# Where the rows 129 to 256 of an expert are divided, and when the last expert's first rows are written, in a second mixture of experts

## The chip, the core and the metric

The kernel runs on one core of one Trainium2 chip. The metric is device time in microseconds (us), the median over runs. One more execution was recorded by the hardware profiler, and all rows below are of it.

## The reference

Attention with two masks (local and strided) gives 1152 rows of 512 numbers. Two mixtures of experts follow. The first sends each row to its two best experts of eight. The second, which the change touches, sends each row to one expert and drops what is over the capacity:

```
expert_idx = np.argmax(logits, axis=1)
...
h = np.maximum(np.einsum('ecd,edf->ecf', disp, w1), 0.0)     # disp: (8, 288, 512), w1: (8, 512, 1024)
y = np.einsum('ecf,efd->ecd', h, w2)                         # w2: (8, 1024, 512)
...
out[i] = gate_w[i] * y[expert_idx[i], pos[i]]
```

How many rows an expert gets is known only when the kernel runs.

## The kernel before

Five engines take part. TensorE (PE) multiplies, ScalarE (ACT) and VectorE (DVE) move and divide data, GpSimd (POOL) issues the gathers and scatters of rows, and SyncE (SP) issues the loads of weights. Each works through its own queue in program order; the order in the code is written out by hand.

**Divided numbers.** To come near fp32 with a faster matmul type, each operand is divided into a high part `hi` and a remainder `lo`, and each product is three matmuls: hi x hi, lo x hi, hi x lo (`mm3`, line 905). For the weights, ACT writes `hi` (line 77) and DVE writes `lo` (line 82), after which SP may load the chunk six places further on into the freed buffer (line 68). For the gathered rows, `x_turn` (line 411) transposes them on PE into a PSUM bank, and `x_split` (line 421) divides the bank: ACT writes `hi` (line 423), then DVE writes `lo` (line 424), both into the tile `xt`.

**Blocks.** An expert's rows come in blocks of 128, 128 and 32 (`nb2`). `block(e, b, ...)` (line 934) is one block's two layers, 24 matmuls of 512 columns for each (`up` and `down`), with a transposition of the hidden layer between them (`h_turn`, lines 918, 920, 921). Block 0 is always computed. Blocks 1 and 2 stand in an If at line 997 and one at line 1004, and are computed where the expert has more than 128 or 256 rows. Every engine passes these Ifs on its own. Where a block is skipped, each engine still steps the semaphores that the block would have stepped. In this run the experts 1, 2, 4 and 7 have a block 1, and expert 2 has a block 2; 0, 3, 5 and 6 have block 0 alone.

**Order in the common part.** `first_block(e)` (line 955) holds what is done for every expert. Between the two layers PE turns the rows of this expert's block 1 into bank 5 and those of the next expert's block 0 into bank 6. In the second layer, at step 2, ACT and DVE divide the next expert's block 0 (line 981). At the steps 3 to 6 they divide four chunks of the next expert's weights (line 983). This expert's block 1 is divided only inside the If (line 998), so that in the queues of ACT and DVE it stands behind those four chunks. For the last expert there are no four chunks.

**Writing.** `put_rows(e, b, ps)` (line 923) scales a block's rows on ACT (line 925), clears a spacer on POOL (line 926) and scatters the rows to the output with an indirect DMA (line 927). An expert's block 0 is put at the start of the next expert's common part. The last expert's block 0 is put at the very end (line 1017), behind its block 1.

**Expert 0.** Behind its common part DVE decodes the lists of rows (`L2.decode()`, lines 505 to 508), and POOL then gathers the rows of expert 2 (line 1015) into a tile that the trace names `hot`. PE turns these in the common part of expert 1.

Of the kernel before, what the change touches and what calls it, by code (L numbers as in the profile page):

```python
# [21 lines left out]
DM, FF, E = 512, 1024, 8  # L22
# [16 lines left out]
def blocks(n):  # L39
    return [(a, min(128, n - a)) for a in range(0, n, 128)]  # L40
# [3 lines left out]
def attention_moe_moe_kernel(ctx: ExitStack, tc: tile.TileContext, a, out, capacity):  # L44
# [35 lines left out]
    def split_lo(i, eng):  # L80
        if i < len(chunks):
            eng.tensor_tensor(lo[i % SPLIT], raw[i % RAW], hi[i % SPLIT].bitcast(F32), op=OP.subtract)  # L82
            load(i + RAW)

    def split(eng=None):
        split_lo(split_hi(), eng or dve)
# [261 lines left out]
    bank = [banks[:, i] for i in range(8)]  # L348
# [30 lines left out]
    def count_ranks(sb, first, last):  # L379

        ps = bank[7][:, :(NT + 1) * E].rearrange("p (c e) -> p c e", e=E)
        pe.matmul(ps[:, :NT, :], tri, sb, start=first, stop=False, skip_group_check=True)
        pe.matmul(ps[:, NT, :], ones, sb[:, NT - 1, :], start=False, stop=False,
                  skip_group_check=True)
        for c in range(NT - 1):
            n = NT - c
            pe.matmul(ps[:, c + 1:NT + 1, :], ones, sb[:, c, None, :].to_broadcast([128, n, E]),
                      start=False, stop=last and c == NT - 2, skip_group_check=True)
        return ps
# [14 lines left out]
    def gather(xg, src, ix, n, only=(0, 1, 2)):  # L404
        for b, (s0, m) in enumerate(blocks(n)):
            if b not in only:
                continue
            pool.indirect_dma_start(out=xg[:m, b, :src.shape[1]], out_offset=None, in_=src,  # L408
                                    in_offset=bass.IndirectOffsetOnAxis(ap=ix[:m, b:b + 1], axis=0))

    def x_turn(xg, b, m, ps=None):
        ps = (ps or next_bank("tr")).rearrange("p (d s) -> p d s", d=4)
        for d in range(4):
            pe.transpose(ps[:, d, :m], xg[:m, b, d * 128:(d + 1) * 128], ident[:m, :m])  # L414
        return ps

    def x_cols(xg, xs, b, m, s0=None, ps=None):

        x_split(x_turn(xg, b, m, ps), xs, b * 128 if s0 is None else s0, m)

    def x_split(ps, xs, s0, m):
        h, l = (x[:, :, s0:s0 + m] for x in xs)
        act.copy(h, ps[:, :, :m])  # L423
        dve.tensor_tensor(l, ps[:, :, :m], h.bitcast(F32), op=OP.subtract)
# [110 lines left out]
    ps = count_ranks(ohb[:, 1], False, True)  # L535
# [311 lines left out]
    nb2 = blocks(c2)  # L847
# [7 lines left out]
    xs2, hs2 = ([t[:, :, i * c2:(i + 1) * c2] for i in range(2)] for t in (xt, ht))  # L855
# [34 lines left out]
    def has(e, b):  # L890
        return (more_blocks >> (2 * e + b - 1)) & 1

    def tell(e, b):
        tc.mark_branch_hint_location(f"block{e}_{b}", hint=has(e, b), engines=engines)  # L894

    pending = [split_hi() for _ in range(4)]
    ps = []
# [25 lines left out]
    def put_rows(e, b, ps):  # L923
        m = nb2[b][1]
        act.activation(rows[e % 2][:m, b, :DM], ps[:m], AF.Copy, scale=L2.g(e, b, m))  # L925
        pool.memset(spacer, 0.0)  # L926
        i = pool.indirect_dma_start(  # L927
            out=out, out_offset=bass.IndirectOffsetOnAxis(ap=L2.ix[:m, e, b:b + 1], axis=0),
            in_=rows[e % 2][:m, b, :DM], in_offset=None, bounds_check=T - 1, oob_is_err=False)
        for k in put:  # L930
            tc.declare_no_dep(i.ins, k.ins, reason="rows of other tokens")
        put.append(i)

    def block(e, b, out_bank, also):

        ci = 64 + 8 * e
        s0, m = nb2[b]
        x, hc = ([t[:, :, s0:s0 + m] for t in u] for u in (xs2, hs2))
        also("start")
        for j in range(2):  # L940
            ps = bank[2 + j]
            for k in range(4):
                mm3(ps[:m], [t[:, k] for t in x], wide(ci + 2 * j, k), k == 0, k == 3)
                if j and k == 1:
                    also("up")
                    h_turn(b, 0)
            act.activation(h[:m, j * 512:j * 512 + 512], ps[:m], AF.Relu)
        also("between")
        for k in range(8):
            mm3(out_bank[:m], [t[:, k] for t in hc], wide(ci + 4, k), k == 0, k == 7)  # L950
            if k == 1:
                h_turn(b, 1)
            also(k)

    def first_block(e):
        def two(n=2):
            for _ in range(n):
                if e == 0 and pending:
                    split_lo(pending.pop(0), dve)
                else:  # L960
                    split()

        def also(at):
            if at == "start":
                if e:
                    two()
                    put_rows(e - 1, 0, bank[0] if e % 2 else bank[7])
                    if e + 2 < E:
                        gather(xg[(e + 2) % 3], acc, L2.ix[:, e + 2], c2)
            elif at == "up":  # L970
                if e:
                    two(1)
            elif at == "between":
                if e:
                    two(1)
                if len(nb2) > 1:
                    s.append(x_turn(xg[e % 3], 1, nb2[1][1], bank[5]))
                if e + 1 < E:
                    s.append(x_turn(xg[(e + 1) % 3], 0, nb2[0][1], bank[6]))
            elif at == 2 and e + 1 < E:  # L980
                x_split(s[-1], xs2, 0, nb2[0][1])
            elif at in (3, 4, 5, 6) and e + 1 < E:
                two(1)

        s = []
        block(e, 0, bank[7] if e % 2 else bank[0], also)
        return s[0] if len(nb2) > 1 else None

    def other_blocks(e, ps):

        def also(at):
            if at == "between" and len(nb2) > 2:
                x_cols(xg[e % 3], xs2, 2, nb2[2][1], ps=bank[6])

        if len(nb2) == 1:
            return
        with tc.If(has(e, 1) > 0, preferred_fallthrough_block=True, label=f"block{e}_1"):  # L997
            x_split(ps, xs2, 128, nb2[1][1])
            if len(nb2) > 2:
                tell(e, 2)  # L1000
            block(e, 1, bank[5], also)
            put_rows(e, 1, bank[5])
            if len(nb2) > 2:
                with tc.If(has(e, 2) > 0, preferred_fallthrough_block=True, label=f"block{e}_2"):  # L1004
                    block(e, 2, bank[6], lambda at: None)
                    put_rows(e, 2, bank[6])

    put = []
    for e in range(E):
        if len(nb2) > 1:  # L1010
            tell(e, 1)
        ps = first_block(e)
        if e == 0:
            L2.decode()
            gather(xg[2], acc, L2.ix[:, 2], c2)
        other_blocks(e, ps)
    put_rows(E - 1, 0, bank[7])


_NAMES = {"w1": "moe_w1", "w2": "moe_w2", "v1": "moe2_w1", "v2": "moe2_w2"}  # L1020
# [96 lines left out]
```

## Time and profile before

| | us |
|---|---|
| runs without the profiler, median of 3 | 554.35 (553.63 to 555.62) |
| the profiled execution's own time | 556.55 |
| its span, first to last instruction | 554.7 |
| PE busy in the span | 509.5 (92%) |
| second mixture, first matmul of block 0 of expert 0 to last of block 1 of expert 7 | 352.7 to 542.8 |

Times in rows are counted from the start of the span. A row of the timeline has its start, its duration (of several equal instructions together, with their count as x2), engine, line, operation and operands; in brackets stands how long the engine was idle before it, and what ended that. An engine's name with a q (ACTq, POOLq) is its sequencer. The ends of matmuls are modelled and overlap; from start to start of two matmuls is the better measure. PEclk is the granted clock of PE as a share of 2.4 GHz: 1.00, or 0.50, which is 1.2 GHz.

### The profile page before, as it was taken

Reading aid. Unit: us, or ns where it says so; the run is one execution under the profiler, and the core shown is the slowest. Engines: PE = TensorE matmul, PEld = TensorE weight load, DVE = VectorE, ACT = ScalarE, POOL = GpSimd, SP = SyncE. Lnnn points to the kernel's source line nnn. Section 1 sums busy time; section 2 is a strip of 40 time slices with the busy share of each in tenths; the row PEclk is TensorE's granted clock in tenths of the full one; section 3 lists DMA queues with packets and bytes.
Section 4 is the critical chain, followed back from the end, with each engine's and each line's share of the span. In section 5 each row is a group of like instructions: output and inputs, shape, how many; then the busy total and the mean of one; then the engine's idle time right before and its main releaser. Section 6 shows DMA issues by size and latency. Waiting matters only on the chain. (4 is left out here: it accounts for less than half of the span.)

```text
span 554.7 us, 9506 instructions
## 1 busy us (share of the span) xinstructions
PE 509.5 (92%) x3367; PEld 434.8 (78%) x3367; DVE 297.1 (54%) x662; ACT 269.5 (49%) x520; POOL 166.6 (30%) x216
## 2 busy tenths in 40 slices
PE   6899779999999999999999999897989999899991
PEld 3777569999999999999999995665767577677770
DVE  5498458755555555555554546175171068348820
ACT  4487345544544636454454623254371177257810
POOL 1244047826123050605030126753040043041001
PEclk9699858999999999999999996998997999899996
DMA  9988666847767576847666474359082069449400
GB/s 198 212 253 248 240 205 216 294 151 188 232 174 224 210 205 209 205 152 169 202 150 168 140 198 69 91 211 327 33 269 109 20 218 353 157 143 331 159 1 20
DMA packets 40669, 102.02 MB, mean 184 GB/s; under 512 B 12209, under 2 KB 12913, under 8 KB 40610
## 3 DMA queue, kind: packets, MB, share of 16 engines
q1 hardware_dynamic: 31506, 84.00, 47.6%
q0 software_dynamic: 7936, 17.24, 12.9%
q8 instruction: 32, 0.52, 0.4%
q14 instruction: 27, 0.22, 0.1%
q10 hardware_dynamic: 1168, 0.04, 0.1%
HBM read 85.93 MB, written 16.26 MB: 184 GB/s over the span
## 5 line engine op out<-in xcount | busy, mean ns | idle before, releaser
L82 DVE TENSOR_TENSOR lo<-raw,hi 128x1024 fp32r<-128x1024 f32 x128 | 153.7, 1223 | 71.2 <-ACT hi L77 64.1
L77 ACT ACTIVATE hi<-raw 128x1024 fp32r<-128x1024 f32 x128 | 131.3, 1056 | 11.1 <-DVE at L478 4.0
L584 PE MATMUL banks<-xt,hi 128*128 128x304 f32 x512 | 118.9, 312 | 1.5 <-ACT xt L423 1.2
L584 PE MATMUL banks<-ht,hi 128*128 128x304 f32 x512 | 110.1, 307 | 0.0
L584 PEld LDWEIGHTS banks<-xt,hi 128*128 128x128 f32 x512 | 87.5, 191 | 5.7 <-issue 4.0
L907 PE MATMUL banks<-hi,xt 128*128 128x512 f32 (+1 forms) x208 | 72.6, 428 | 14.6 <-ACT xt L423 5.4
L632 POOL DMA_INDIRECT acc<-rows,to x24 | 40.7, 1695 | 148.6 <-issue 68.1
L584 PEld LDWEIGHTS banks<-ht,hi 128*128 128x128 f32 x512 | 83.2, 188 | 0.4
L584 PE MATMUL banks<-ht,lo 128*128 128x304 f32 x256 | 77.3, 302 | 0.0
L584 PE MATMUL banks<-xt,lo 128*128 128x304 f32 x256 | 74.0, 306 | 0.0
L907 PE MATMUL banks<-hi,ht 128*128 128x512 f32 (+1 forms) x208 | 68.0, 407 | 0.2 <-issue 0.2
L907 PEld LDWEIGHTS banks<-hi,xt 128*128 128x128 f32 (+1 forms) x208 | 39.1, 195 | 29.4 <-ACT xt L423 7.0
L591 ACT ACTIVATE ht<-banks 128x304 fp32r<-128x304 f32 x64 | 27.1, 424 | 55.5 <-PE banks L584 53.6
L927 POOL DMA_INDIRECT out_dram<-rows,ix x13 | 14.3, 1100 | 129.0 <-POOLq L1004 65.9
L921 DVE TENSOR_TENSOR ht<-banks,ht 128x512 fp32r<-128x512 f32 (+1 forms) x26 | 17.1, 658 | 60.1 <-ACT ht L920 49.6
L584 PEld LDWEIGHTS banks<-xt,lo 128*128 128x128 f32 x256 | 49.3, 192 | 0.0
L584 PEld LDWEIGHTS banks<-ht,lo 128*128 128x128 f32 x256 | 48.2, 188 | 0.0
L592 DVE SCALAR_TENSOR_TENSOR ht<-banks,ht 128x304 fp32r<-128x304 f32 x64 | 29.9, 470 | 31.8 <-ACT ht L591 30.8
L907 PEld LDWEIGHTS banks<-hi,ht 128*128 128x128 f32 (+1 forms) x208 | 35.9, 182 | 10.8 <-DVE ht L921 1.5
L907 PE MATMUL banks<-lo,xt 128*128 128x512 f32 (+1 forms) x104 | 43.1, 415 | 0.0
L423 ACT CAST xt<-banks 128x512 fp32r<-128x512 f32 (+2 forms) x40 | 20.0, 501 | 45.1 <-PE banks L414 29.7
L907 PE MATMUL banks<-lo,ht 128*128 128x512 f32 (+1 forms) x104 | 41.0, 394 | 0.0
(166 smaller groups left out, 667.4 us busy)
## 6 DMA issues: line engine op xcount, KB each, us to landing
raw<-w SPq DMA_DIRECT2D x64, 512.0 KB
raw<-v SPq DMA_DIRECT2D x64, 512.0 KB
acc<-zero SPq DMA_DIRECT2D x4, 780.0 KB
sqk<-sqk SPq DMA_DIRECT2D x4, 630.0 KB
x_dram<-xr SPq DMA_DIRECT2D x9, 256.0 KB
out_dram<-zero SPq DMA_DIRECT2D x3, 768.0 KB
lv<-lv SPq DMA_DIRECT2D x4, 432.0 KB
sv<-sv SPq DMA_DIRECT2D x4, 315.0 KB
```

The lines of the kernel that those rows point to most:

```text
L77: act.activation(hi[i % SPLIT], raw[i % RAW], AF.Copy)
L82: eng.tensor_tensor(lo[i % SPLIT], raw[i % RAW], hi[i % SPLIT].bitcast(F32), op=OP.subtract)
L423: act.copy(h, ps[:, :, :m])
L584: pe.matmul(ps, w[k], x[i][:, k, :n], start=j == 0, stop=j == len(terms) - 1)
L591: act.activation(hs[0][:, f, :n], ps, AF.Relu)
L592: dve.scalar_tensor_tensor(hs[1][:, f, :n], ps, 0.0, hs[0][:, f, :n].bitcast(F32), op0=OP.max, op1=OP.subtract)
L632: i = pool.indirect_dma_start(out=acc, out_offset=bass.IndirectOffsetOnAxis(ap=L1.to[:m, e, b:b + 1], axis=0), in_=rows[e % 2][:m, b, :], ...
L907: pe.matmul(ps, stat[s], mov[x], start=first and j == 0, stop=last and j == 2)
L921: dve.tensor_tensor(hl, ps, hh.bitcast(F32), op=OP.subtract)
L927: i = pool.indirect_dma_start(out=out, out_offset=bass.IndirectOffsetOnAxis(ap=L2.ix[:m, e, b:b + 1], axis=0), in_=rows[e % 2][:m, b, :DM] ...
```

## The change

The block 1 of an expert is divided at step 2 of the second layer of its block 0, for every expert, ahead of the next expert's block 0 and of the four weight chunks; the division inside the If goes. In the last expert, block 0 is put after its common part and ahead of the If.

```diff
-            elif at == 2 and e + 1 < E:
-                x_split(s[-1], xs2, 0, nb2[0][1])
+            elif at == 2:
+                if len(nb2) > 1:
+                    x_split(s[0], xs2, 128, nb2[1][1])
+                if e + 1 < E:
+                    x_split(s[-1], xs2, 0, nb2[0][1])
             elif at in (3, 4, 5, 6) and e + 1 < E:
                 two(1)
...
-        return s[0] if len(nb2) > 1 else None
-
-    def other_blocks(e, ps):
+
+    def other_blocks(e):
...
         with tc.If(has(e, 1) > 0, preferred_fallthrough_block=True, label=f"block{e}_1"):
-            x_split(ps, xs2, 128, nb2[1][1])
             if len(nb2) > 2:
                 tell(e, 2)
             block(e, 1, bank[5], also)
...
-        ps = first_block(e)
+        first_block(e)
         if e == 0:
             L2.decode()
             gather(xg[2], acc, L2.ix[:, 2], c2)
-        other_blocks(e, ps)
-    put_rows(E - 1, 0, bank[7])
+        elif e == E - 1:
+            put_rows(e, 0, bank[7])
+        other_blocks(e)
```

## Rows read from the trace of the kernel before

**Rows 1.** The page: PE's busy time, and its costliest group that waits.

```profile
PE 509.5 (92%) x3367; PEld 434.8 (78%) x3367; DVE 297.1 (54%) x662; ACT 269.5 (49%) x520; POOL 166.6 (30%) x216
...
L907 PE MATMUL banks<-hi,xt 128*128 128x512 f32 (+1 forms) x208 | 72.6, 428 | 14.6 <-ACT xt L423 5.4 <-DVE xt L424 4.6 <-ACTq L997 2.4
```

**Rows 2.** Who waited for whom, 365 to 545 us: total, times, longest.

```profile
PE banks L907 <- DVE xt L424: 4.4, 3, 1.5
...
PE banks L907 <- ACT xt L423: 3.7, 3, 1.2
...
PE banks L907 <- ACTq L997: 2.4, 3, 0.8
```

**Rows 3.** Timeline, all engines, between block 0 and block 1 of expert 4.

```profile
472.65 0.50 PE L907 MATMUL banks<-hi,xt 128*128 128x512 f32 x1 [1.23 <-ACT xt L423]
...
473.86 0.68 DVE L424 TENSOR_TENSOR xt<-banks,xt 128x512 fp32r<-128x512 f32 x1
474.60 0.79 PE L907 MATMUL banks<-hi,xt 128*128 128x512 f32 x1 [1.45 <-DVE xt L424]
```

**Rows 4.** Windows: block 1 of experts 1, 2, 4, 7, with the wait ahead.

```profile
382.32:399.60 17.28, 14.60 (x61) 10.99 (x60) 4.96 (x7) 3.86 (x7) 0.00 (x0) 0.90 0.35 127
413.67:432.24 18.57, 15.91 (x62) 12.06 (x61) 4.95 (x7) 3.84 (x7) 0.00 (x0) 0.82 0.33 116
471.26:488.46 17.20, 14.52 (x61) 10.94 (x60) 4.96 (x7) 3.86 (x7) 0.00 (x0) 0.90 0.36 130
530.06:542.69 12.63, 12.63 (x61) 9.77 (x59) 1.67 (x3) 2.53 (x5) 0.00 (x0) 1.00 0.00 0
```

The columns are the window, its length, the busy time (and count) of PE, PEld, DVE, ACT and POOL, then PEclk, the DMA engines' share and GB/s.

**Rows 5.** Windows: the stretches at the low clock, and 8 us of block 1.

```profile
385.45:388.86 3.41, 3.20 (x8) 2.55 (x9) 0.16 (x1) 0.00 (x0) 0.00 (x0) 0.50 0.86 329
416.17:422.99 6.82, 5.99 (x14) 4.75 (x15) 0.77 (x2) 0.60 (x1) 0.00 (x0) 0.50 0.57 214
474.19:477.61 3.42, 3.01 (x7) 2.43 (x8) 0.36 (x1) 0.00 (x0) 0.00 (x0) 0.50 0.87 341
...
480.00:488.00 8.00, 8.00 (x42) 6.26 (x41) 1.68 (x3) 1.93 (x4) 0.00 (x0) 1.00 0.01 2
```

**Rows 6.** Timeline of PE, from block 0 to block 1 of expert 7.

```profile
529.83 0.39 PE L907 MATMUL banks<-lo,ht 128*128 128x512 f32 x1
530.06 0.63 PE L907 MATMUL banks<-hi,xt 128*128 128x512 f32 x2
```

**Rows 7.** Timelines of ACT and PE at skipped Ifs, experts 3 and 0.

```profile
453.73 0.59 ACT L423 CAST xt<-banks 128x512 fp32r<-128x512 f32 x1
454.20 3.91 ACT L77 ACTIVATE hi<-raw 128x1024 fp32r<-128x1024 f32 x4
...
458.21 0.74 PE L907 MATMUL banks<-hi,xt 128*128 128x512 f32 x2 [0.79 <-ACTq L997]
...
367.45 0.72 PE L907 MATMUL banks<-hi,xt 128*128 128x512 f32 x2 [0.55 <-PEq L997]
```

**Rows 8.** Timelines of DVE, POOL and PE: lists and rows of expert 2.

```profile
364.54 4.62 DVE L82 TENSOR_TENSOR lo<-raw,hi 128x1024 fp32r<-128x1024 f32 x4
369.52 0.18 DVE L505 CAST ix<-lst 128x24 int32<-128x24 f32 x1 [0.36 <-DMA lst<-list]
...
370.48 1.02 POOL L408 DMA_INDIRECT hot<-acc,ix  x1 [4.14 <-DVEq L997]
...
375.79 0.66 PE L414 MATMUL banks<-ident,hot 128*128 128x128 f32 x4 [1.62 <-DMA hot<-acc,ix]
```

**Rows 9.** Timeline of POOL at the end, and two lines' sequencer instructions.

```profile
543.85 0.98 POOL L927 DMA_INDIRECT out_dram<-rows,ix  x1 [21.98 <-POOLq L1004]
...
546.37 0.98 POOL L927 DMA_INDIRECT out_dram<-rows,ix  x1 [0.74 <-issue]
...
L1004 POOLq INC_SWDGE_SEM  x1: 1403/1403/1403, 543.9 to 543.9; - x1
...
L1113 POOLq DRAIN  x3: 50/115/7665, 546.1 to 554.4; - x3
```

The last two have a count, the minimum, median and maximum duration in ns, and the first and last start.

## The prediction

> **What bounds the kernel now.** I read the page first. PE is busy for 92% of the span, and its costliest waiting group is the first layer's matmuls: it names x divided on ACT, x divided on DVE, and ACT's passing of line 997 [rows 1]. So PE bounds, and what matters is where PE stands still. The view of who waited for whom puts that on places: three waits for ACT's x, three for DVE's x, three for ACT at the skipped If [rows 2]. The timeline at expert 4 shows the first two kinds as one event: PE stands 1.23 us until ACT has divided block 1, issues one matmul, and stands 1.45 us more until DVE has divided it, although PE turned that bank long before [rows 3]. Experts 1 and 2 show the same pair. The windows of the four blocks 1 give the whole cost: 17.28, 18.57 and 17.20 us with the wait, 12.63 us in expert 7, where no weight chunks stand ahead of the division [rows 4]. The idle time is not all of that. Behind the two waits the granted clock falls to 0.50, for 3.41, 6.82 and 3.42 us; in expert 7's block it stays at 1.00 [rows 4, 5].
>
> **The change part by part.**
>
> *Division ahead of the four splits, experts 1, 2 and 4.* PE's work is unchanged; x is ready some 4 us before PE needs it, because ACT's four chunk splits (3.91 us in expert 3's part [rows 7]) now come behind it. Expert 7 shows what is left: block 1 starts 0.23 us after the last matmul of block 0, one matmul's pitch, so the If costs a PE that waits for nobody no time [rows 6]. I take 12.63 us for each block: 17.28 + 18.57 + 17.20 - 3 x 12.63 = 15.16 us saved. Of that, idle time is (3.7 + 4.4) = 8.1 us [rows 2], and the halved clock 13.65 / 2 = 6.8 us [rows 5]; together 14.9, so the two readings agree. ACT and DVE finish their chunks 0.47 and 0.68 us later. In expert 4 that is still before block 1's first half of the first layer (12 matmuls of 0.23 us) is done for ACT, and before the first hidden transposition (18 matmuls) for DVE: zero, covered by those matmuls. SP's four loads go out up to 0.68 us later too; late in the block the DMA engines are at 0.01 [rows 5], so there is room: zero. In the experts without block 1 the buffers that were loaded ahead cover it, as no wait of a weight split for a load is among the waits that I found; without that cover it costs those 0.68 us each.
>
> *The same division, now also in experts 0, 3, 5 and 6.* There the If held it and was skipped; now it is work. On ACT it is a pitch of 0.47 us (453.73 to 454.20 [rows 7]), ahead of four splits. What is behind them is the skipped If: PE's next block starts at 458.21, released by ACT's passing it, whose last split ended at 454.20 + 3.91 = 458.11 [rows 7]. There are three such waits [rows 2]; each grows by the full 0.47: +1.41 us. In expert 0 PE itself comes last [rows 7], so nothing. The bounds are 0 and 3 x 0.68 = 2.0 us, if DVE became the later one.
>
> *Expert 0's lists.* On DVE the added division takes up to 0.68 us [rows 3] ahead of four splits that ended at 364.54 + 4.62 = 369.16; they end at 369.84, and the decoding, which began at 369.52 when its list landed, is 0.32 us late. POOL's gather waits for it, and PE waits 1.62 us for the gathered rows [rows 8]. Cost between 0 (if the busy DMA engines set the landing) and 0.32; I take 0.32, as every link of that chain waits for the one ahead.
>
> *The last expert's block 0 put earlier.* ACT's scaling moves into expert 7's idle time ahead of block 1's first result, and POOL's spacer and scatter move there too. ACT's scaling waits for the end of block 0 (530.06 [rows 6]); behind it on ACT stands only block 1's first result, 12 matmuls of PE later, and behind the scatter on POOL only block 1's own, 12 us later. At the end, the second scatter (546.37) goes and the first (543.85) is the last [rows 9]: at most 2.52 us. POOL's closing drain starts at 546.14 and lasts 7.67, to 553.81, 6.46 after the second scatter's 0.98 us are over [rows 9]. If it follows POOL's last work, that is now the skipped If's semaphore step, 543.90 + 1.40 = 545.30: it ends at 551.76, 2.05 us saved. If its length is fixed, the saving is 546.14 - 545.30 = 0.84 at most. I take 2.05, because the drain outlasts every other thing in the trace and so must follow something on POOL. Nothing is added behind the last block, so no loss.
>
> *Sum.* -15.16 - 2.05 + 1.41 + 0.32 = -15.5 us. Of the profiled execution's own 556.55 (span 554.7) that leaves 541.1. That execution is 2.2 us above the median of the runs; I subtract the same from the median: 554.35 - 15.5 = 538.9.
>
> *The clock's share.* The same pair of waits was followed by 3.41, 6.82 and 3.42 us at 1.2 GHz [rows 5], so this term is not tied to the wait's length. If all three stretches are short in the usual run, the term is 5.1 and the time 540.6; if all are long, 10.2 and 535.5. The Trainium skill, in "TensorE: Matmul & The Clock Gate", section "What's actually happening", says that the number of matmuls at the low clock differs from run to run for one kernel. The trace agrees as far as one execution can, with two lengths for one pattern.
>
> **The rivals.**
>
> *The clock falls elsewhere.* PE's wait for expert 2's rows grows to 1.94 us, and three joins from 0.79 to 1.26 us [rows 2, 7, 8]. If a fall moves to one, it takes back 1.7 us (half of 3.41) or 3.4. For it: two waits of 1.2 and 1.5 us were enough. Against it: 1.62 us alone left the clock at 1.00, and PE is now busier around it. With one short and one long fall: 538.9 + 5.1 = 544.0. Chance 0.08.
>
> *The If costs PE time that the wait for x hid.* Expert 7 entered without a gap, but its queue had other things ahead. The nearest row for an If without another engine's wait is expert 0's skipped one, 0.55 us idle [rows 7]. Three times that: 540.6. Chance 0.10. The Trainium skill, in "Runtime: NRT & Kernel Launch", section "Instruction fetch mechanics", says that a taken branch outside the loaded window stalls until its code is fetched. By that rule the entry could cost more than a pitch; expert 7's 0.23 us [rows 6] speaks against it where the block is entered, and no row shows the other three.
>
> *Slower: the wait only changes its name.* At the skipped Ifs PE is released by ACT only after all four splits [rows 7]. If PE's first matmul of block 1 waited likewise for the last weight split on ACT and then on DVE, the change would not do what it says: the three blocks would keep their times, since the order of five operations changes and not their sum. Then 1.41 + 0.32 are paid and the end gives 0.84: 555.2; with one of the two short clock stretches coming out long (+1.7), 556.9. It decides if the three blocks give back less than 0.3 us each. Against it: PE's two waits name x alone [rows 2, 3], and the weights of block 1 were divided an expert earlier. Chance 0.03.
>
> **How the numbers follow.** The forecast, 538.9, has 0.79: no wait is left ahead of block 1, by the same operation that expert 7 shows. The range takes the long clock stretches on one side (535.5) and, on the other, short stretches with the small saving at the end (540.6 + 1.2 = 541.8), the costly If, and a single fall of the clock elsewhere (542.3 if long): 535.5 to 542.5. About 0.3%, 1.7 us, is what a measurement of this kernel can tell from no change; every case but the last is faster by more. Faster 0.95, same 0.03 and slower 0.02 divide that last case and leave a little for what I have not seen.
>
> **What would show it.** Right: the three windows of block 1 at about 12.6 us with PEclk 1.00; no PE wait that names x; the joins at 1.2 to 1.3 us idle; four more divisions at lines 423 and 424; one scatter behind expert 7's block 1, and the drain's end about 6.5 us after the last semaphore step. Wrong: a PE gap at a block 1 that names another releaser, a PEclk of 0.50 between 375 and 530 us, or weight splits that wait for loads.

## The result and the profile after

The changed kernel takes **536.44 us** (median of 4, 535.3 to 538.68) where the kernel before takes 553.99 beside it (552.31 to 555.62): a ratio of 0.9688 [0.9642, 0.9735], 17.5 us faster. The forecast was 538.9. The profiled execution took 538.68 (span 536.9), against 556.55 (554.7) before. The sections below compare these two spans, 17.8 us apart.

The page of the changed kernel: busy times, and the first layer's waiting group. Line 997 is now line 999.

```profile
PE 501.4 (93%) x3367; PEld 431.0 (80%) x3367; DVE 299.5 (56%) x666; ACT 271.3 (51%) x524; POOL 170.4 (32%) x216
...
L907 PE MATMUL banks<-hi,xt 128*128 128x512 f32 (+1 forms) x208 | 67.2, 404 | 6.2 <-ACTq L999 3.8
```

Against [rows 1], x is gone from the releasers, both from ACT and from DVE; what is left is the skipped If, with 3.8 us where it had 2.4. PE's count is the same and its busy time 8.1 us less, 7.1 of it in the blocks 1 of the experts 1, 2 and 4: the same matmuls, there with PEclk at 1.00 where it was 0.82 to 0.90 [rows 4]. ACT and DVE have four instructions more each, the divisions of the experts 0, 3, 5 and 6.

The windows of block 1 of the experts 1, 2, 4 and 7 in the changed kernel (columns as in [rows 4]):

```profile
381.04:393.68 12.64, 12.64 (x61) 9.77 (x59) 4.86 (x6) 3.89 (x7) 0.61 (x2) 1.00 0.60 220
407.72:420.34 12.62, 12.62 (x61) 9.89 (x60) 4.82 (x6) 3.85 (x7) 0.00 (x0) 1.00 0.46 171
459.85:472.48 12.63, 12.63 (x61) 9.77 (x59) 4.86 (x6) 3.88 (x7) 0.00 (x0) 1.00 0.54 186
515.05:527.68 12.63, 12.63 (x61) 9.78 (x59) 1.68 (x3) 3.22 (x6) 1.05 (x2) 1.00 0.05 21
```

All four are alike now, with PE busy to the end and PEclk 1.00. The first three had 17.28, 18.57 and 17.20.

Timeline of PE in the changed kernel, between block 0 and block 1 of expert 4, where [rows 3] had two stalls:

```profile
459.62 0.39 PE L907 MATMUL banks<-lo,ht 128*128 128x512 f32 x1
459.85 0.63 PE L907 MATMUL banks<-hi,xt 128*128 128x512 f32 x2
```

From the last matmul of block 0 to the first of block 1 it is 0.23 us, one matmul's pitch, as in expert 7 before [rows 6]. The pitch is 0.23 us at the entries of experts 1 and 2 as well. The Trainium skill's rule on taken branches ("Runtime: NRT & Kernel Launch", section "Instruction fetch mechanics"), which I had put beside the rival of a costly If, does not show at these entries. They are a weak test of it: the kernel asks for the entered block as the fall-through, and no trace shows that a branch is taken there.

What it costs stands at the skipped Ifs. Timelines of ACT and PE in the changed kernel at expert 3, to be laid beside [rows 7]:

```profile
441.83 1.08 ACT L423 CAST xt<-banks 128x512 fp32r<-128x512 f32 x2
442.79 3.92 ACT L77 ACTIVATE hi<-raw 128x1024 fp32r<-128x1024 f32 x4
...
446.81 0.73 PE L907 MATMUL banks<-hi,xt 128*128 128x512 f32 x2 [1.28 <-ACTq L999]
```

ACT divides two blocks instead of one ahead of the four splits, and PE, which waits for ACT's passing of the If, is idle 1.28 us instead of 0.79.

The end: the last scatters on POOL in the changed kernel, and the sequencers' rows for the drain and for the skipped If's step.

```profile
516.22 0.98 POOL L927 DMA_INDIRECT out_dram<-rows,ix  x1 [9.34 <-ACT rows L925]
...
528.84 0.98 POOL L927 DMA_INDIRECT out_dram<-rows,ix  x1 [11.56 <-POOLq L1005]
...
L1005 POOLq INC_SWDGE_SEM  x1: 1423/1423/1423, 528.9 to 528.9; - x1
...
L1115 POOLq DRAIN  x3: 46/109/5556, 530.5 to 536.6; - x3
```

Block 0 of expert 7 is scattered 12.6 us ahead of block 1, so one scatter is left behind the last matmul where [rows 9] had two.

The difference, by stretches of the two traces (from the first issue of a stretch to the first of the next):

| stretch | before | after | difference |
|---|---|---|---|
| blocks 1 of experts 1, 2, 4, with the gap ahead | 53.05 | 37.89 | -15.16 |
| gaps at the skipped Ifs of experts 3, 5, 6 | 3.55 | 5.02 | +1.47 |
| last matmul's issue to the end of the span | 12.2 | 9.45 | -2.75 |
| start of the span to the last matmul of block 0 of expert 1 | 382.1 | 380.8 | -1.3 |

The sum is -17.7 of the 17.8. The last line lies ahead of all that the change moves but expert 0's division, and is taken up below. Behind it, the rest of the kernel (called so from here on) takes 172.56 us before and 156.07 after. The rest is what the experiments compare, since the first stretch varied between 377.7 and 385.3 us over 14 profiles with no order by kernel. What the change costs at expert 0's list lies in that first stretch, so the rest does not show it.

### The profile page after: what moved, and what is told of

Its sections match the earlier page's. It is cut to its first block, busy times and chain, and to the rows that moved or that the text cites. A ratio compares the mean times of both kernels' runs of the same rounds, so it can differ in the third digit from the quotient of the medians.

```text
span 536.9 us, 9519 instructions
## 1 busy us (share of the span) xinstructions
PE 501.4 (93%) x3367; PEld 431.0 (80%) x3367; DVE 299.5 (56%) x666; ACT 271.3 (51%) x524; POOL 170.4 (32%) x216
## 3 DMA queue, kind: packets, MB, share of 16 engines
q0 software_dynamic: 7936, 17.24, 13.1%
## 5 line engine op out<-in xcount | busy, mean ns | idle before, releaser
L907 PE MATMUL banks<-hi,xt 128*128 128x512 f32 (+1 forms) x208 | 67.2, 404 | 6.2 <-ACTq L999 3.8
L907 PEld LDWEIGHTS banks<-hi,xt 128*128 128x128 f32 (+1 forms) x208 | 36.3, 182 | 17.8 <-ACTq L999 5.1
L423 ACT CAST xt<-banks 128x512 fp32r<-128x512 f32 (+2 forms) x44 | 21.8, 513 | 40.0 <-PE banks L414 34.5
L907 PE MATMUL banks<-lo,xt 128*128 128x512 f32 (+1 forms) x104 | 41.1, 395 | 0.0
```

The source lines that it names most:

```text
L907: pe.matmul(ps, stat[s], mov[x], start=first and j == 0, stop=last and j == 2)
```

## Experiments

All compute the full result. The diffs are against the changed kernel. Kernels sent together share a chip and the runs of the kernel before.

### One part of the change without the other

Division ahead, last expert's block 0 put at the very end again:

```diff
-        elif e == E - 1:
-            put_rows(e, 0, bank[7])
         other_blocks(e)
+    put_rows(E - 1, 0, bank[7])
```

> Division early as in the changed kernel, last expert's block 0 put at the very end as before. Theory (the two parts are independent, and the closing drain follows the last scatter): the windows of block 1 of experts 1, 2, 4 stay at 12.63 us, and the stretch from the last matmul's issue to the end of the span goes back from 9.45 to 12.2 us; 2.7 us slower than the changed kernel, 14 to 15 faster than before, about 539.2. Rival (the drain has its length whatever stands ahead of it): under 1 us slower than the changed kernel, about 537.3.

Measured: 539.65 (538.11 to 543.4) beside 553.4, ratio 0.9787 [0.9726, 0.9849]. The last matmul to the end takes 12.18 us, 2.7 more than in the changed kernel, and the rest 158.82, 2.75 more. POOL's scatters and drain in this kernel:

```profile
527.43 0.98 POOL L927 DMA_INDIRECT out_dram<-rows,ix  x1 [21.97 <-POOLq L1005]
...
529.95 0.98 POOL L927 DMA_INDIRECT out_dram<-rows,ix  x1 [0.74 <-issue]
...
L1114 POOLq DRAIN  x3: 46/115/7663, 529.7 to 537.9; - x3
```

The second scatter is back, 2.52 us behind the first, and the long drain with it. So the end is worth 2.75 us once the division stands ahead.

The other half: put early, division inside the If.

```diff
             elif at == 2:
-                if len(nb2) > 1:
-                    x_split(s[0], xs2, 128, nb2[1][1])
...
         with tc.If(has(e, 1) > 0, preferred_fallthrough_block=True, label=f"block{e}_1"):
+            x_split(ps, xs2, 128, nb2[1][1])
```

> Only the last expert's block 0 is put earlier, the division stays in the If. Theory: the stretch from the last matmul's issue to the end is 9.45 us instead of 12.2, all else as before: 2.7 us faster than before, about 551.3, with the two waits ahead of block 1 and the low clock still there (windows 17 to 19 us). Rival (drain of fixed length): 0.8 us faster, about 553.2.

Measured: 552.71 beside 553.4, ratio 0.9993 [0.9962, 1.0025]: no measurable gain, where 2.7 us were expected. That is a miss, and the trace tells why. The end did shrink, to 9.6 us. But ahead of it, expert 7's block 1 starts late. ACT and PE in this kernel there:

```profile
526.78 0.69 ACT L925 ACTIVATE rows<-banks,lst 128x512 f32<-128x512 f32 x1 [3.63 <-PE banks L907]
527.37 0.58 ACT L423 CAST xt<-banks 128x512 fp32r<-128x512 f32 x1
...
528.00 0.50 PE L907 MATMUL banks<-hi,xt 128*128 128x512 f32 x1 [1.25 <-ACT xt L423]
```

Scaling block 0 has to wait for its last matmul, and on ACT's queue the division inside the If now stands behind that scaling. ACT sat idle 3.63 us with x's bank full, and PE then waited for x at the one block where it had not waited before: 2.0 us lost for the 2.6 gained (12.2 to 9.6). The two halves of the change depend on each other: putting early pays only with the division out of the If.

### The place in the queue, or the leaving of the If

If what helps is the place ahead of the weight splits, the division in the common part but behind them must bring nothing, and places between must bring a part. `at == 7` below was 7, 4 and 5 in three kernels: behind all four, two and three of the splits.

```diff
             elif at == 2:
-                if len(nb2) > 1:
-                    x_split(s[0], xs2, 128, nb2[1][1])
...
-            elif at in (3, 4, 5, 6) and e + 1 < E:
-                two(1)
+            elif at in (3, 4, 5, 6, 7):
+                if at < 7 and e + 1 < E:
+                    two(1)
+                if at == 7 and len(nb2) > 1:
+                    x_split(s[0], xs2, 128, nb2[1][1])
```

> As the changed kernel, but the division stands in the common part behind the four weight chunks (step 7) instead of ahead of them. Theory (the place in the queues of ACT and DVE is what counts): the two waits of 1.2 and 1.5 us and the low clock behind them come back, windows 17 to 19 us; the joins at skipped Ifs keep their 0.47 us more; only the early put's 2.7 us are gained: about 1.3 us faster than before, 552.7. Rival (leaving the If is what counts): as the changed kernel, 536.5.

> As the changed kernel, but the division stands behind two of the four weight chunks. Theory (idle time and clock are two terms, and a short wait leaves the clock alone): ACT's half is ready before PE needs it, DVE's half about 0.8 us after; windows of block 1 at 13.4 to 13.6 us with PEclk 1.00; 2.5 us slower than the changed kernel, about 539.0. Rival (any wait at this place lowers the clock): windows of 15 to 17 us with a stretch at 0.50; 7 to 12 us slower than the changed kernel.

> As the changed kernel, but the division stands behind three of the four weight chunks. Behind two, the blocks took 13.57 us with PEclk 1.00; behind four, 17.38 with 3.41 us at 0.50. One more chunk is one more pitch on DVE, 1.16 us. Theory (the clock is a term of its own, that comes in whole or not at all): 14.7 us for each block if it stays, 16.4 if it falls, and nothing between; which of the two, no row tells. Rival (what was called the clock's cost grows smoothly with the wait): about 15.5 for every block, with slow matmuls in proportion.

| division stands behind | time, beside before | ratio |
|---|---|---|
| four splits | 553.72, 553.4 | 1.0023 [0.9992, 1.0054] |
| three | 549.53, 558.23 | 0.9859 [0.9767, 0.9951] |
| two | 538.54, 553.4 | 0.9752 [0.9693, 0.981] |
| none (the change) | 536.44, 553.99 | 0.9688 [0.9642, 0.9735] |

Windows of block 1 of the experts 1, 2 and 4, behind four splits:

```profile
377.92:395.31 17.39, 14.71 (x61) 11.05 (x60) 4.97 (x7) 3.87 (x7) 0.12 (x2) 0.90 0.41 143
409.35:426.64 17.29, 14.63 (x61) 11.10 (x61) 4.94 (x7) 3.84 (x7) 0.00 (x0) 0.90 0.37 127
466.14:483.52 17.38, 14.71 (x61) 11.05 (x60) 4.96 (x7) 3.86 (x7) 0.00 (x0) 0.90 0.38 139
```

The same behind three splits:

```profile
385.57:401.82 16.25, 14.70 (x61) 11.05 (x60) 4.97 (x7) 3.88 (x7) 0.00 (x0) 0.89 0.42 154
415.91:432.19 16.28, 14.76 (x61) 11.17 (x61) 4.95 (x7) 3.86 (x7) 0.00 (x0) 0.90 0.39 132
471.70:486.41 14.71, 13.16 (x61) 9.88 (x60) 4.96 (x7) 3.88 (x7) 0.00 (x0) 1.00 0.45 159
```

And behind two:

```profile
378.60:392.17 13.57, 12.90 (x61) 9.69 (x59) 4.96 (x7) 3.87 (x7) 0.00 (x0) 1.00 0.52 185
...
459.27:472.84 13.57, 12.89 (x61) 9.69 (x59) 4.97 (x7) 3.88 (x7) 0.00 (x0) 1.00 0.45 165
```

Out of the If but behind the four splits, the blocks keep their 17.3 us, and the median is that of before. Of the 1.3 us that the early put was expected to leave as a gain, none shows; the three blocks alone differ by more than that between the two profiles of the kernel before (53.05 and 50.5 us). So the place in the queue is the cause, not the If. Behind two splits a wait of 0.7 us is left and the clock stays. The three windows behind three splits show the clock's part by itself: the waits are the same in all (0.28 and 1.26 us idle), but after two of them the clock fell to 0.50 for 3.41 us, after the third it did not, and the window is 1.6 us shorter. In these windows the clock's part came whole or not at all.

### What the joins cost, and whether it can be had back

At the skipped Ifs PE waits until ACT has passed, behind the added division and four splits. First, the fourth split goes behind the If. It needs the scaling of the expert before moved from the start to between the layers:

```diff
                 if e:
                     two()
-                    put_rows(e - 1, 0, bank[0] if e % 2 else bank[7])
...
                     two(1)
+                    put_rows(e - 1, 0, bank[0] if e % 2 else bank[7])
...
-            elif at in (3, 4, 5, 6) and e + 1 < E:
+            elif at in (3, 4, 5) and e + 1 < E:
...
         other_blocks(e)
+        if e + 1 < E:
+            split()
```

> As the changed kernel, but the fourth weight chunk of the next expert is divided behind the If instead of ahead of it, and the putting of the preceding expert's block 0 moves from the start of the common part to between its layers. Theory (PE's three waits at skipped Ifs are for the last weight split on ACT): the gaps there go from 1.68 us to about 0.95, the gap of expert 0's, where PE comes last; 2.2 us faster than the changed kernel, about 534. Rival (passing the If costs that time itself): gaps of 1.6 to 1.7, no faster, or slower by what ACT now has to do in the next first layer.

Second, the whole of block 1 is divided on DVE, `hi` as well, so that ACT has nothing added:

```diff
-    def x_split(ps, xs, s0, m):
+    def x_split(ps, xs, s0, m, copy=None):
...
-        act.copy(h, ps[:, :, :m])
+        (copy or act.copy)(h, ps[:, :, :m])
...
-                    x_split(s[0], xs2, 128, nb2[1][1])
+                    x_split(s[0], xs2, 128, nb2[1][1], dve.tensor_copy)
```

> As the changed kernel, but DVE writes both halves of block 1's rows; ACT has none of the added work. Theory (the joins grew by ACT's 0.47 us alone): gaps at the three skipped Ifs back from 1.68 to 1.19 us, windows of block 1 still 12.63; 1.4 us faster than the changed kernel, about 535. Rival (DVE is as late as ACT): gaps of 1.6 or more and waits for DVE in the next expert's first layer; the same as the changed kernel or slower.

Measured on one chip, beside 558.23: 538.65, ratio 0.9707 [0.9614, 0.9799], and 540.29, ratio 0.9739 [0.964, 0.9838]. The changed kernel was not run on that chip, so the times do not test the expected 534 and 535; the stretches do. In the first the gaps at the skipped Ifs fell from 1.67 to 0.87, 0.87 and 0.91 us as expected, 2.4 in all; in the second to 1.19, 1.16 and 1.18, those of before. So ACT's queue sets these gaps and the added division is what lengthened them. But the blocks behind them grew: PE's weight loads waited longer for DVE's `ht` (line 921). Who waited for whom from 440 to 530 us, in the changed kernel:

```profile
PEld banks L907 <- DVE ht L921: 1.0, 5, 0.2
```

in the kernel with the fourth split behind the If:

```profile
PE banks L907 <- ACTq L999: 1.0, 2, 0.5
...
PEld banks L907 <- DVE ht L921: 2.0, 8, 0.4
```

and with `hi` on DVE:

```profile
PEld banks L907 <- DVE ht L921: 2.9, 9, 0.8
```

The first keeps about 1.5 of the 2.4 us (rest 154.51 against 156.07). The second keeps 0.3 (155.80), and that lies at the end (9.19 us against 9.45): what the joins gave, 1.5 us, DVE took in the next blocks. There the sum missed, though the gaps came out as forecast.

### The stretch ahead: the lists of expert 2

In the changed kernel block 0 of expert 1 takes 17.2 us, more than any other. DVE and PE there:

```profile
369.92 0.18 DVE L505 CAST ix<-lst 128x24 int32<-128x24 f32 x1 [3.65 <-DMA lst<-list]
...
371.15 0.66 PE L918 MATMUL banks<-ident,yT 128*128 128x128 f32 x4 [2.89 <-ACT yT L947]
...
374.38 0.66 PE L414 MATMUL banks<-ident,hot 128*128 128x128 f32 x4 [0.74 <-DMA hot<-acc,ix]
```

DVE, and ACT beside it, stand still until the list has landed, and PE waits for them. To take these waits out, POOL decodes the list (the two operations of `decode` whose result nobody reads are left out), expert 2's rows are turned and divided later, and ACT scales later:

```diff
-                    put_rows(e - 1, 0, bank[0] if e % 2 else bank[7])
...
                     two(1)
+                    put_rows(e - 1, 0, bank[0] if e % 2 else bank[7])
...
-                if e + 1 < E:
+                if e + 1 < E and e != 1:
                     s.append(x_turn(xg[(e + 1) % 3], 0, nb2[0][1], bank[6]))
...
-                if e + 1 < E:
+                if e + 1 < E and e != 1:
                     x_split(s[-1], xs2, 0, nb2[0][1])
+            elif at == 7 and e == 1:
+                x_cols(xg[2], xs2, 0, nb2[0][1], ps=bank[6])
...
-            L2.decode()
+            pool.tensor_copy(L2.ix, L2.sb[:, :, :, 0])
```

> As the changed kernel, but expert 2's list is decoded on POOL instead of DVE, expert 2's rows are turned and divided at the last step of expert 1's block 0, and the putting of the preceding expert's block 0 moves to between the layers. Theory (block 0 of expert 1 takes 17 to 20 us instead of 12.8 because ACT and DVE wait for the list ahead of work that PE needs, and this wait swallows whatever time the stages ahead won): it takes 12.9 to 13.5 us, 4 us faster than the changed kernel, about 532.5. Rival (the rows of expert 2 land too late whatever waits for them): the same 17 us, the wait now at the last step or ahead of expert 2.

Measured: 538.61 beside 558.23, ratio 0.9677 [0.9588, 0.9765]. Window of that block in this kernel:

```profile
367.45:380.38 12.93, 12.85 (x60) 10.16 (x61) 10.93 (x12) 9.85 (x13) 8.42 (x8) 1.00 0.98 349
```

The wait is gone, 4.3 us of this block against the changed kernel's profile; 0.4 of that comes back behind the block, where expert 2's rows are now turned. Three edits were made at once, and no run tells which of them was needed. The forecast of about 532.5 us was missed: the ratio is that of the change itself on other chips, and block 0 of expert 0, which the edit does not touch, took 3.4 us longer here (taken up in the next section).

### The changed kernel again, and both improvements together

> The changed kernel once more, beside the next one on the same chip. Theory (the three blocks, the joins and the end are fixed terms; what stands ahead of expert 1's block 1 varies from run to run): blocks of 12.63 us, gaps of 1.68 us at three skipped Ifs, 9.45 us from the last matmul's issue to the end, a ratio to before between 0.964 and 0.974; block 0 of expert 1 anywhere from 14.5 to 20 us, longer where the second mixture starts earlier. Rival (that block's wait belongs to the change): always about 17 us.

> The changed kernel with both further edits: the fourth weight chunk behind the If, and expert 2's list decoded on POOL with its rows turned at the last step of expert 1's block 0. Theory (the two are independent): gaps of 0.87 to 0.91 us at the skipped Ifs, from the first matmul of expert 1's block 0 to the last of its block 1 about 25.8 us instead of 27 to 30, together 3 to 5 us faster than the changed kernel on the same chip. Rival (the wait for the list only moves to where the rows of expert 2 are needed): 1.5 us faster, by the joins alone.

Measured beside 553.56: the changed kernel 544.39 (541.73 to 547.38), ratio 0.9862 [0.9817, 0.9908]; the kernel with the fourth split behind the If and the lists on POOL 535.52 (533.38 to 539.58), ratio 0.9698 [0.965, 0.9746]. On this chip the change gave 9.2 us between the medians (7.6 by the ratio), not 17.5, although its rest is 155.93 us as always: a miss, as 0.964 to 0.974 was expected. Its profile is longer than the first one ahead of the rest: block 0 of expert 0 took 16.79 us from first to last matmul (13.34 in the first profile). Who waited for whom there, in this execution:

```profile
DVE early L441 <- remote: 6.2, 1, 6.2
...
ACT ht L920 <- remote: 4.2, 1, 4.2
ACT xt L423 <- remote: 4.1, 1, 4.1
```

The timeline of the same:

```profile
360.04 0.60 PE L918 MATMUL banks<-ident,yT 128*128 128x128 f32 x4
...
362.79 0.58 ACT L920 CAST ht<-banks 128x512 fp32r<-128x512 f32 x1 [4.16 <-remote]
363.43 0.50 PE L907 MATMUL banks<-hi,ht 128*128 128x512 f32 x1 [1.38 <-ACT ht L920]
```

PE's transposes were over at 360.6; ACT, which reads what they wrote, starts 2.2 us later (0.04 us in the first profile of the changed kernel), and the view names none of this kernel's instructions as what ended the wait. That is about half of the 3.4 us. The other half is the clock, which stood at 0.50 from the start of this block:

```profile
350.12:353.53 3.41, 3.21 (x8) 2.45 (x8) 1.46 (x2) 0.00 (x0) 2.92 (x5) 0.50 0.50 106
```

Block 0 of expert 0 took 16.7 to 16.8 us in all six profiles of two chips: this one, and that of the kernels with both edits, the division behind three splits, the fourth split moved, `hi` on DVE and the lists on POOL. In five of them ACT is 1.9 to 2.3 us late and the clock is at 0.50 for 3.41 us; with the lists on POOL ACT is 0.8 us late, and 6.5 us at 0.50 make up nearly all of the difference. On the other chips the block took 13.3 to 13.8, whatever the kernel, and the clock did not fall in it. Late signals alone do not explain the small gain: the other chip where they showed gave ratios of 0.9677 to 0.9739 for three near kin of the changed kernel.

Then comes expert 2's list. DVE and PE in this execution, and the clock behind them:

```profile
365.21 4.62 DVE L82 TENSOR_TENSOR lo<-raw,hi 128x1024 fp32r<-128x1024 f32 x4
369.75 0.17 DVE L505 CAST ix<-lst 128x24 int32<-128x24 f32 x1
...
376.17 0.66 PE L414 MATMUL banks<-ident,hot 128*128 128x128 f32 x4 [2.00 <-DMA hot<-acc,ix]
...
377.42:380.84 3.42, 3.42 (x12) 2.74 (x11) 0.56 (x1) 1.18 (x3) 2.51 (x4) 0.50 1.01 372
```

Here DVE goes from its four splits to the list without a pause: its queue, and not the landing, sets the decoding (ACT's scaling at 369.01, which reads the same list, did not wait for it either). Two divisions take 1.28 us on DVE where one takes 0.68, so by my estimate about 0.6 us of PE's wait of 2.00 us for expert 2's rows is the change's, and behind that wait the clock fell for 3.4 us. Whether it would have fallen behind the shorter wait, no run shows.

The kernel with both edits shows the same late signals and is 8.9 us faster than the changed kernel beside it, where 3 to 5 were expected. Of that, the profiles show 1.3 in the rest (154.64) and 4.1 in block 0 of expert 1 (12.48 from first to last matmul, against 16.56); what is left, 3.5 us, no view accounts for. The two profiled executions are only 3.3 us apart (541.73 and 538.39), as the second mixture began 1.9 us later in that of the combined kernel; the other runs left no trace. Against the changed kernel beside it, the combined kernel is the faster one, though its ratio to before is no better than the change's on other chips.

### Both kernels on one more chip

> The kernel before, profiled on the same chip as the next run, because the changed kernel gained 3.1% on one chip and 1.4% on another, where PE's signals to ACT ahead of expert 0's second layer were followed 2.2 us late and the clock fell in block 0 of expert 1. Theory (those late signals belong to the chip or the execution, and hit both kernels): they show here as well; from the last matmul of expert 1's block 0 to the end of the span 170 to 173 us. Rival (the changed kernel alone pays for them): none here, and the stretch up to that matmul 4 to 8 us shorter than the changed kernel's.

> The changed kernel, profiled on the same chip as the run above. Theory: from the last matmul of expert 1's block 0 to the end 155.9 to 156.1 us, as twice before, and the stretch up to it within 2 us of the kernel before's; ratio 0.965 to 0.975. Rival: the stretch up to it 4 to 8 us longer than the kernel before's, ratio 0.98 to 0.99.

Measured beside 551.02: the kernel before 551.07 (548.19 to 557.6), ratio 0.9999 [0.9959, 1.004]; the changed kernel 537.18 (531.18 to 537.96), ratio 0.970 [0.9641, 0.976]. The rest is 170.01 and 155.93 us: 14.1 us, beside 13.8 between the medians (16.5 by the ratio; the profiled execution of the changed kernel was the slowest of its six). Neither kernel shows the late signals of the section before, so the expectation that they would hit both kernels here went untested, and whether the kernel before has them on those two chips stays open. Windows of block 1 of the experts 1, 2 and 4 in this profile of the kernel before:

```profile
379.36:396.83 17.47, 14.72 (x61) 11.05 (x60) 5.04 (x7) 3.87 (x7) 0.00 (x0) 0.90 0.41 146
410.95:428.16 17.21, 14.55 (x62) 11.05 (x61) 4.95 (x7) 3.84 (x7) 0.00 (x0) 0.90 0.38 124
467.15:482.99 15.84, 13.16 (x61) 9.88 (x60) 4.96 (x7) 3.86 (x7) 0.00 (x0) 1.00 0.39 150
```

The same two waits as in [rows 4] (expert 4 too starts 1.62 us late), but the clock fell for 3.4 us twice and the third time not at all. Against 12.63 each, these blocks hold 12.6 us, where the first profile had 15.2.

## Why the prediction was right, point by point

**The three blocks: right.** They were forecast at 12.63 us each and came out at 12.62 to 12.64: -15.16, to the digit, against this one execution. The cover that was named held: no wait of PE in block 1 names a chunk split, and none names x.

**The clock's share: right in kind.** The term was given as 5.1 to 10.2 us by whether the stretches come short or long. The runs show that a stretch can also be missing (expert 4 in the last profile of the kernel before and, at 15.84 us, in that of the put alone; the third block behind three splits). So the lower bound should have been 0 for each, and the 6.8 us that the forecast took were one draw of several. With what the last profile shows, the blocks were worth 12.6 us on that chip. Had that profile been the one on record, the same sum would have given about 541.4 (an estimate: 554.35 - 12.6 - 2.05 + 1.41 + 0.32), so part of how near the forecast came is luck. What the forecast cited of the Trainium skill ("TensorE: Matmul & The Clock Gate", section "What's actually happening"), that the number of slow matmuls differs from run to run, is borne out more strongly than by the first trace: 0, 3.41 and 6.82 us behind one pattern of waits in the middle of a kernel, where the page's counts are for a kernel's start.

**The joins: right.** +1.41 forecast, +1.47 measured (1.17 to 1.19 before, 1.66 to 1.68 after; idle 1.28 where 1.2 to 1.3 was named). That ACT's queue sets them was shown from both sides: with a split less they fall to 0.87, without the added division to 1.18.

**Expert 0's list: the step that failed in the first profile, and not in all.** I took +0.32, as "every link of that chain waits for the one ahead". In the first profile of the changed kernel DVE is through with its splits 3.65 us before it can go on with the list (2.85 on the last chip), so the landing sets the decoding, and the added division costs nothing there. Where the kernel was run again first, DVE did not wait at all, and the chain held as forecast: there the cost was about 0.6 us by the estimate above, twice what I took, and possibly the clock's fall with it. In [rows 8] DVE had waited only 0.36 us for the list; in the second profile of the kernel before it waited 5.42. So the term is 0 or more by how early DVE gets to the list, and one row could not tell. What this stretch did, -1.3 us, is not the change's: on the last chip the changed kernel reached the same matmul 1.0 us later than the kernel before (380.15 and 379.13).

**The end: mechanism right, size off.** -2.05 forecast, -2.75 measured, beyond the upper bound of 2.52. The step that failed is that POOL's last work "is now the skipped If's semaphore step". That step ran from 528.9 to 530.3 in the changed kernel, and the drain ended at 536.06: 5.75 us behind it, not 6.46. Against the end of the last scatter's 0.98 us it is 6.24 (before: 6.46; with the division alone: 6.46). Over the 14 profiles the drain ended 5.96 to 6.47 us behind the last scatter; where the step came last it ended 5.5 to 6.0 behind the step, and never the forecast 6.46. So the step does not set the end and the last scatter comes nearer, though what the drain waits for is not shown. The whole 2.5 us of the second scatter's place went, and 0.2 more; in the other profiles with block 0 put early the stretch is 9.17 to 9.70 us, a saving of 2.5 to 3.0. Alone, this edit gave nothing, which the prediction did not see: it called what stands behind the scaling on ACT "only block 1's first result", true only because the division had left the If.

**The rivals.** The clock fell nowhere in the joins or in PE's wait for the list in the changed kernel's first profile; where it was run again first, it did fall behind PE's wait for expert 2's rows, the place that the first rival named, and there the added division was part of the wait. It is not the change's doing alone: in the second profile of the kernel before the clock fell in the same block, which took 18.6 us there. The If cost no PE time. The wait did not merely change its name; it would have done so behind the four splits, where the kernel stayed at 17.3 us a block.

**The sum.** -15.16 - 2.75 + 1.47 = -16.4, and -1.3 ahead of it that belongs to the execution, make the 17.7 between the profiles. The medians gave 17.5, 13.8 and 9.2 us on three chips (17.3, 16.5 and 7.6 by the ratios). The traces of both kernels account for 17.8 and 13.1 us between the profiled executions of the first two, with 2.5 us of the difference in the three blocks, by the clock, and 2.3 us ahead of the rest. The 9.2 stay open beyond the list and the clock behind it: the profiled execution of the changed kernel was the fastest of its six runs there, and the kernel before was not profiled on that chip.

## What to carry to other kernels

In a queue that runs in order, put the short operation that the bottleneck engine waits for ahead of bulk work that is not due yet, and look at what the bulk's consumers then lack: here 1.5 us came back at the joins. Price a stall of TensorE as idle time plus what the clock may add, and treat the latter as a term that comes or does not, from more than one profile. Test the halves of a change alone: one of them may open the wait that the other one closes.

## What was not expected of the hardware

- The clock's answer to a stall does not follow from the stall's length alone: behind 1.2 and 1.5 us of waiting it stayed at 2.4 GHz, or was at 1.2 GHz for 3.41 or 6.82 us; behind 0.28 and 1.26 us likewise, it fell twice and once not.
- ACT took up PE's results 1.9 to 2.3 us after PE's work had ended in five of the six executions profiled on two chips (0.8 us in the sixth), and 0.04 us after in the first profile (block 0 of expert 0). The changed kernel was profiled both ways.
- POOL's closing drain ended 5.96 to 6.47 us after the last scatter's own time in 14 profiles, also where other work of POOL came behind that scatter.
